# Filling empty TensorE slots with matmuls on a zero tile until the second weight has arrived

## The chip, the cores and the metric

One core of a Trainium2 chip. The metric is the device time of one execution in microseconds (us), the median of several. The profile's span is measured from the first to the last instruction on that core; in the profiled runs here the device time is 1.7 to 2.0 us above it.

Every ratio of two kernels below is the mean time of one kernel's fast runs over the mean time of the other's fast runs in the same rounds on the same chip, so it is not quite the ratio of the medians that are quoted. Brackets hold its 95% interval. A run counts as slow when it is over 1.5% above the fastest run of its kernel.

## The reference

A gated linear recurrence feeds a feed-forward layer with a squared ReLU. Inputs and output are float32.

```python
# q, k, v, alpha: [4 batches, 8 heads, 768 steps, 48]
for t in range(S):
    state = alpha[:, :, t, :, None] * state + einsum('bhd,bhe->bhde', k[:, :, t], v[:, :, t])
    y[:, :, t] = einsum('bhd,bhde->bhe', q[:, :, t], state)
x = y as [3072 tokens, 384]
out = square(relu(x @ w_in)) @ w_out        # w_in [384, 2048], w_out [2048, 384]
```

## The kernel before

The sequence is cut into 24 chunks of 128 steps. A chunk's attention needs four loads (alpha, k, q, v) and a chain across engines: decay sums on TensorE, exponentials on ScalarE, scaled q and k on VectorE, transposes, scores, mask, result, transposition into `XT`. The feed-forward layer takes blocks of chunks: `s1` (into `psH`, weight `WIN`), ReLU on ScalarE, squares shared by VectorE and GpSimd, and `s2` (into `psO`, weight `WOUT`), in four groups of four matmuls per chunk.

No order of instructions is written by hand. The program records operations with a cost, a priority and dependences. A list scheduler inside the kernel plays them through with a small model of the engines and of the two load queues, and its order is what each engine executes, with waits where they are needed.

```python
SHARE = {"sp": 0.25, "pool": 0.75}     # how two load queues share the DMA, in the scheduler's model
...
# GpSimd's queue: four chunks of w_in, then eight of w_out; w_out chunk i is issued when
# the alpha of attention chunk i+1 has landed
W_OUT_FROM = 2
if W_OUT_FROM <= g < W_OUT_FROM + NWO:
    i = g - W_OUT_FROM
    wo_dma[i] = add("pool", w_out_dma(i), 800, -1e4 + i, writes=[("wout", i)], ...,
                    lag=1230, after=[raw_dma[g - 1, "a"]])
...
# s2: four groups of four matmuls; group s needs two of the eight w_out chunks
add("pe", s2, pe_ns(*[DM] * 4), ps_, reads=[("gt", gt, u) for u in us] +
    [("wout", i) for i in range(s * NWO // 4, (s + 1) * NWO // 4)], writes=[("ps", "O")], ...)
# ScalarE copies psO into one of NOSB = 3 output buffers; the out transfer stands in the
# same queue (SP) as the input loads
add("act", lambda e, ob=ob: e.activation(OSB[ob][:], psO[:, 0:DM], AF.Copy), ...,
    reads=[("ps", "O")], writes=[("osb", ob)], name=f"oe{g}")
add("sp", lambda e, ob=ob, r0=r0: e.dma_start(out[r0:r0 + C, :], OSB[ob][:]), 350, ps_ + 1300,
    reads=[("osb", ob)], ...)
```

## Time and profile before

| | before |
|---|---|
| median time | 208.03 us (207.96 to 208.54) |
| span of the profiled run | 204.8 us (this run took 206.55 us, 1.5 us under the median) |
| TensorE busy | 181.4 us, 89% |
| from 60.27 to 202.0 us | TensorE busy 140.44 of 141.73 us |
| clock granted, mean | 0.967 |

How to read it: a high busy share over the whole span hides two regimes, one with holes and one without. The prediction below shows the lines.

### The profile page before, as it was taken

How to read it: one execution, taken by the hardware profiler on the slowest of the kernel's cores; microseconds unless marked ns; L12 is line 12 of the kernel's file. 1: busy time of each engine (PE TensorE's matmuls, PEld its weight loads, DVE VectorE, ACT ScalarE, POOL GpSimd, SP SyncE). 2: the span in 40 equal slices, each digit the busy share in tenths (PEclk: the TensorE clock that was granted, in tenths of full speed). 3: DMA queues.
4: the chain of work that ended last, by engine and by line, in shares of the span. 5: the costliest groups of instructions: out<-in, count | busy, mean ns of one | idle time of the engine just before them, and what ended most of it. 6: DMA issues, size and time to landing. Idle time of an engine off the chain costs nothing.

```text
span 204.8 us, 4675 instructions
## 1 busy us (share of the span) xinstructions
PE 181.4 (89%) x1940; PEld 136.0 (66%) x1940; DVE 110.8 (54%) x175; ACT 111.4 (54%) x237; POOL 89.4 (44%) x113
## 2 busy tenths in 40 slices
PE   1375597698699999999999999999999999999984
PEld 0275486486576677777767778778777786777752
DVE  4433546578875536835274575656845847643200
ACT  3125336467585446743574846756847657455540
POOL 8305325249565227324624446626527334223440
PEclk9999559799999999999999999999999999999999
DMA  6999999999999999999497394081011110110112
GB/s 129 167 198 184 182 219 223 200 206 194 211 187 178 207 192 214 196 229 241 113 191 158 82 226 118 17 180 38 3 38 42 38 42 0 43 38 0 42 38 77
DMA packets 107093, 27.04 MB, mean 132 GB/s; under 512 B 100416, under 2 KB 107072, under 8 KB 107072
## 3 DMA queue, kind: packets, MB, share of 16 engines
q1 hardware_dynamic: 103296, 23.60, 53.5%
q0 software_dynamic: 3776, 3.15, 10.6%
q8 instruction: 15, 0.25, 0.5%
q14 instruction: 6, 0.05, 0.1%
HBM read 25.17 MB, written 4.72 MB: 146 GB/s over the span
## 4 chain that ended last, share of the span: by engine, by line
PE 78%; DVE 6%; DMA 6%; ACT 5%; issue 1%; POOL 1%; DVEq 0%; ACTq 0%
PE psO L540 30%; PE psH L518 30%; PE psT L424 6%; DMA wout<-in_moe_w_out_dram 5%; PE psP L436 4%; DVE qks L414 3%; PE psY L452 2%; PE psT L487 2%; DVE pm L441 2%; PE psY L449 1%; DMA raw<-in_alpha_dram 1%; ACT rr L524 1%; PE psA L392 1%; PE psY L465 1%; ACT asb L403 1%
## 5 line engine op out<-in xcount | busy, mean ns | idle before, releaser
L528 POOL TENSOR_TENSOR gt<-rr 128x512 bf16<-128x512 bf16 x48 | 50.2, 1046 | 82.8 <-ACT rr L524 81.5
L524 ACT ACTIVATE rr<-psH 128x512 bf16<-128x512 f32 x96 | 57.4, 599 | 49.3 <-PE psH L518 46.4
L540 PE MATMUL psO<-wout,gt 128*128 128x384 bf16 x384 | 78.2, 330 | 1.4 <-ACT osb L547 0.9
L518 PE MATMUL psH<-xt,win 128*128 128x256 bf16 (+1 forms) x624 | 78.1, 275 | 0.2
L518 PEld LDWEIGHTS psH<-xt,win 128*128 128x128 bf16 x624 | 58.5, 104 | 10.9 <-DVE xt L493 0.5
L540 PEld LDWEIGHTS psO<-wout,gt 128*128 128x128 bf16 x384 | 34.1, 98 | 18.3 <-ACT osb L547 1.4
L528 DVE TENSOR_TENSOR gt<-rr 128x512 bf16<-128x512 bf16 x48 | 22.9, 477 | 27.8 <-ACT rr L524 27.6
L441 DVE TENSOR_TENSOR pm<-psP,ltri 128x1024 bf16<-128x1024 f32 x24 | 29.4, 1223 | 9.1 <-PE psP L436 9.0
L414 DVE TENSOR_TENSOR qks<-raw,asb 128x768 bf16<-128x768 f32 x24 | 25.3, 1057 | 13.6 <-ACT asb L405 13.5
L430 DVE COPY kqt<-psT 128x1024 bf16<-128x1024 bf16 x24 | 16.5, 690 | 9.5 <-PE psT L424 9.0
L493 DVE COPY xt<-psT 128x384 bf16<-128x384 bf16 x24 | 8.5, 355 | 23.9 <-PE psT L487 23.9
L411 POOL CAST vbf<-raw 128x384 bf16<-128x384 f32 x24 | 14.2, 594 | 15.3 <-PE psY L465 9.2
L424 PE MATMUL psT<-ident,qks 128*128 128x128 bf16 x192 | 16.0, 231 | 5.4 <-DVE qks L414 4.2
L424 PEld LDWEIGHTS psT<-ident,qks 128*128 128x128 bf16 x192 | 12.9, 104 | 8.2 <-DVE qks L414 4.5
L547 ACT ACTIVATE osb<-psO 128x384 f32<-128x384 f32 x24 | 11.8, 492 | 11.3 <-PE psO L540 11.0
L459 ACT ACTIVATE xbf<-psY 128x384 bf16<-128x384 f32 x24 | 11.9, 496 | 11.1 <-PE psY L452 11.1
L481 POOL TENSOR_TENSOR sbd<-tmp,acm 128x384 bf16<-128x384 f32 x16 | 14.4, 903 | 6.6 <-DVE tmp L479 6.6
L403 ACT ACTIVATE asb<-psA 128x384 bf16<-128x384 f32 x24 | 11.8, 490 | 9.3 <-PE psA L396 8.2
L388 ACT ACTIVATE lab<-raw 128x384 bf16<-128x384 f32 x24 | 12.9, 538 | 4.0 <-DMA raw<-in_alpha_dram 4.0
L436 PE MATMUL psP<-kqt 64*128 64x128 bf16 x192 | 10.2, 229 | 2.6 <-DVE kqt L430 2.6
L392 PE MATMUL psA<-lab,ltri 128*128 128x384 bf16 x24 | 8.2, 342 | 4.6 <-ACT lab L388 4.4
L452 PE MATMUL psY<-vbf,pm 128*128 128x48 bf16 x192 | 9.0, 186 | 3.4 <-DVE pm L441 3.4
(36 smaller groups left out, 110.5 us busy)
## 6 DMA issues: line engine op xcount, KB each, us to landing
raw<-in_alpha_dram SPq DMA_DIRECT2D x24, 192.0 KB, 4.2
raw<-in_k_dram SPq DMA_DIRECT2D x24, 192.0 KB, 4.0
raw<-in_q_dram SPq DMA_DIRECT2D x24, 192.0 KB, 3.9
raw<-in_v_dram SPq DMA_DIRECT2D x24, 192.0 KB, 4.1
out_dram<-osb SPq DMA_DIRECT2D x24, 192.0 KB, 2.3
win<-in_moe_w_in_dram POOLq DMA_DIRECT2D x4, 384.0 KB, 8.6
wout<-in_moe_w_out_dram POOLq DMA_DIRECT2D x8, 192.0 KB, 4.6
```

Of the source, the lines that this page charges most:

```text
L403: add("act", lambda e: e.activation(ASB[a][:, 0, :], psA[:, 0:HD], AF.Exp, scale=-1.0), act_ns(HD), p0 + 500, reads=[("ps", "A")], writes= ...
L411: add("pool", lambda e: e.tensor_copy(VBF[vb][:], RAW[r][:, 2, :]), 500, p0 + 600, reads=[("raw", r, 2)], writes=[("vbf", vb)], name=f"vc{g}")
L414: add("dve", lambda e: e.tensor_tensor(QKS[qs][:, :, :, 0:D], RAW[r][:, 0:2, :].rearrange("p j (h d) -> p j h d", h=H), ASB[a][:, :, :].re ...
L424: ins = pe.matmul(psT[:, o:o + 128], QKS[qs][:, j, 2 * p:2 * p + 2, :].rearrange("p h d -> p (h d)"), IDENT[:], is_transpose=True)
L430: add("dve", lambda e: e.tensor_copy(KQT[kt][:].rearrange("p j n s -> p (j n s)"), psT[:, :]), dve_ns(1024, 2), p0 + 3000, reads=[("ps", " ...
L436: ins = pe.matmul(psP[:, h, p * 128:(p + 1) * 128], KQT[kt][64 * h:64 * h + 64, 0, p, :], KQT[kt][64 * h:64 * h + 64, 1, p, :])
L441: add("dve", lambda e: e.tensor_tensor(PM[pm][:].rearrange("p j n s -> p (j n) s"), psP[:, :, :].rearrange("p j (n s) -> p (j n) s", n=NPR ...
L481: add("pool", lambda e: e.tensor_tensor(sb3, TMP[g % 2][:].rearrange("p (n d) -> p n d", d=D), acm, ALU.mult), 800, p0 + 8000, reads=[("tm ...
L518: ins = pe.matmul(psH[hb][:, i * n:(i + 1) * n], WIN[:, kk, fj * 128:(fj + 1) * 128], XT[:, kk, g0 * C:g0 * C + n], start=(kk == 0), stop= ...
L524: add("act", lambda e, hb=hb, rb=rb: e.activation(RR[rb][:], psH[hb][:], AF.Relu), act_ns(512), pu + 600, reads=[("ps", "H", hb)], writes= ...
L528: add(eng, lambda e, rb=rb, dst=dst: e.tensor_tensor(dst, RR[rb][:].rearrange("p (i s) -> p i s", i=per), RR[rb][:].rearrange("p (i s) -> ...
L540: ins = pe.matmul(psO[:, 0:DM], GT[gt][:, fj, ti * C:(ti + 1) * C], WOUT[:, fj, :], start=(fj == 0), stop=(fj == FT - 1))
```

## The change

The intent: in the profile before, TensorE's clock fell to half after stretches of 3.41 us in which it was 35% and 46% busy (the prediction shows them), and the start of the kernel is full of short waits. Matmuls on a zero tile, into `psO`, which nothing uses yet, should keep the clock up. They are placed by the scheduler wherever TensorE is free and nothing is ready, as long as TensorE was busy for less than half of the last 3.4 us, and up to the first `s2`. So that this stretch lasts until the second weight is complete, the first `s2` now waits for all eight chunks of it. Three constants of the scheduler's model changed too.

```diff
-    SHARE = {"sp": 0.25, "pool": 0.75}
+    SHARE = {"sp": 0.15, "pool": 0.85}
...
+            if kind == "w" and cold:                       # every 100 ns of the scheduler's time
+                heapq.heappush(events, (now + 100, -1, "w", None))
+                recent = [(a, z) for a, z in recent if z > now - 3400]
+                used = sum(z - max(a, now - 3400) for a, z in recent)
+                if free["pe"] <= now and not avail["pe"] and used < share * 3400:
+                    o = make_warm()
+                    ...                                    # runs now, 216 ns
...
+                    if e == "pe":
+                        recent.append((o.start, o.end))
+                        cold = cold and o.name != last_use
...
+    WARM = nc.alloc_sbuf_tensor("warm", [128, 512], BF16)
+    warmed = add("dve", fill(WARM, 0.0), 200, -3e6, writes=[("warm",)], name="warm")
+    def make_warm():
+        o = Op("pe", lambda pe: pe.matmul(psO[:, 0:512], WARM[:, 0:128], WARM[:]), 216, 0, "w")
...
+    pr.warm = (make_warm, 1000.0, "s2_0_0", 0.5)
...
-    (input loads)  lag=880
+    (input loads)  lag=800
-    reads=[...] + [("wout", i) for i in range(s * NWO // 4, (s + 1) * NWO // 4)]
+    reads=[...] + [("wout", i) for i in range(NWO)]
-    (w_in loads)   lag=2450
+    (w_in loads)   lag=2400
```

Three parts, then: **ZERO** (the zero matmuls), **WAIT** (all of wout before the first `s2`) and **ORDER** (the model's constants, which change nothing on the chip but the order).

More of the change, by code (lines that the diff above doesn't have):

```diff
@@ L39, in __init__ @@
         self.dma_count = {}
+        self.warm = None
     def add(self, eng, fn, cost, prio, reads=(), writes=(), name="", dma=None, lag=0, after=()):
@@ L101, in schedule @@
         tick = 0
+        recent = []
+        cold = self.warm is not None
+        if cold:
+            make_warm, warm_from, last_use, share = self.warm
+            heapq.heappush(events, (warm_from, -1, "w", None))
         def rates():
@@ L122, in schedule @@
             moved = kind in "qm"
+            if kind == "w" and cold:
[4 more added lines that the diff above has]
+                    o = make_warm()
+                    o.start, o.end = now, now + o.cost
+                    o.pos = len(order["pe"])
+                    order["pe"].append(o)
+                    self.ops.append(o)
+                    free["pe"] = o.end
+                    recent.append((o.start, o.end))
+                    done += 1
+                    heapq.heappush(events, (o.end, seq, "f", o))
+                    seq += 1
             if kind == "r":
@@ L151, in schedule @@
                     done += 1
+                    if e == "pe":
+                        recent.append((o.start, o.end))
+                        cold = cold and o.name != last_use
                     if o.sem is not None:
@@ L331, in select @@
                                          pattern=pattern, channel_multiplier=mult)
+    warmed = add("dve", fill(WARM, 0.0), 200, -3e6, writes=[("warm",)], name="warm")
+    def make_warm():
+        o = Op("pe", lambda pe: pe.matmul(psO[:, 0:512], WARM[:, 0:128], WARM[:]), 216, 0, "w")
+        o.deps[warmed] = True
+        o.idx = -1
+        return o
+    pr.warm = (make_warm, 1000.0, "s2_0_0", 0.5)
     for i, t in enumerate(LAB):
@@ L384, in attention @@
             raw_dma[g, nm] = add("sp", lambda e, dst=dst, src=src: e.dma_start(dst, src), 650, p0 - 3 * P + o,
-                                 writes=[("raw", r, j)], name=f"ld{nm}{g}", dma=f"{nm}{r}", lag=880, after=held(g))
+                                 writes=[("raw", r, j)], name=f"ld{nm}{g}", dma=f"{nm}{r}", lag=800, after=held(g))
         lab = LAB[la][:, :, 0:D]
@@ L544, in moe @@
                 us = range(s * nu // 4, (s + 1) * nu // 4)
-                add("pe", s2, pe_ns(*[DM] * 4), ps_, reads=[("gt", gt, u) for u in us] + [("wout", i) for i in range(s * NWO // 4, (s + 1) * NWO // 4)],
+                add("pe", s2, pe_ns(*[DM] * 4), ps_, reads=[("gt", gt, u) for u in us] + [("wout", i) for i in range(NWO)],
                     writes=[("ps", "O")], name=f"s2_{g}_{s}")
@@ L559, in bass_gla_recurrent__then__act_relu_squared_kernel @@
                 wi_dma[i] = add("pool", w_in_dma(i), 800, -1e6 + 3, writes=[("win", i)], name=f"wi{i}", dma=f"wi{i}",
-                                lag=2450)
+                                lag=2400)
         if W_OUT_FROM <= g < W_OUT_FROM + NWO:
```

## The prediction

> **What bounds the kernel now.** I read the page's slices first (its second part), to see where TensorE is full and what clock it was granted. In the slices, each digit is a fortieth of the 204.8 us span, 5.12 us.
>
> ```profile
> span 204.8 us, 4675 instructions
> ...
> PE   1375597698699999999999999999999999999984
> ...
> PEclk9999559799999999999999999999999999999999
> DMA  6999999999999999999497394081011110110112
> ```
>
> TensorE (PE) is full from about 60 us to the end. Before that it has holes, and the clock drops to half in two places. DMA is full from 5 us to about 97 us. So there are two regimes: a start that is paced by loads and dependences, and from 60 us a pure TensorE stretch. The wide stretches confirm it (columns: stretch, length, then busy us of PE, PEld, DVE, ACT, POOL with counts, granted clock, DMA share, GB/s):
>
> ```profile
> 12.06:44.71 32.65, 25.13 (x273) 20.02 (x271) 17.77 (x27) 14.52 (x35) 11.09 (x15) 0.79 1.13 204
> 44.71:60.27 15.56, 12.76 (x171) 10.49 (x172) 11.90 (x17) 11.18 (x26) 11.70 (x14) 1.00 1.10 200
> 60.27:202.00 141.73, 140.44 (x1465) 103.34 (x1465) 75.90 (x120) 82.02 (x173) 60.33 (x67) 1.00 0.47 108
> ```
>
> From 60.27 us on TensorE idles 1.3 us in 141.7. What starts this stretch is in the chain of waits: the last chunk of the second weight, issued late by GpSimd.
>
> ```profile
> 53.81 0.47 DVE tmp L479
> 54.29 0.07 issue
> 54.36 0.77 POOL sbd L481
> 55.13 5.09 DMA wout<-in_moe_w_out_dram
> 60.23 0.05 issue
> 60.27 0.82 PE psO L540 x4
> ```
>
> The reader is to see that the end equals the moment at which wout is complete, plus the TensorE work not yet done by then, plus a tail. The tail is 2.8 us (last matmul ends at 202.0, span 204.8).
>
> The clock. I cut the trace along its transitions, which finer stretches put at 20.99, 31.23, 38.06 and 41.47 us:
>
> ```profile
> 17.58:20.99 3.41, 1.20 (x19) 0.85 (x16) 1.40 (x2) 1.64 (x5) 1.89 (x3) 1.00 1.10 195
> 20.99:24.40 3.41, 1.79 (x25) 1.08 (x22) 2.31 (x3) 1.48 (x5) 0.77 (x1) 0.50 1.06 181
> 24.40:27.82 3.42, 2.76 (x26) 2.55 (x27) 2.13 (x4) 0.47 (x1) 1.37 (x2) 0.50 1.21 220
> 34.64:38.06 3.42, 1.57 (x34) 1.16 (x31) 2.67 (x4) 1.52 (x5) 2.36 (x4) 1.00 1.17 201
> 38.06:41.47 3.41, 3.01 (x23) 2.06 (x21) 1.11 (x3) 1.26 (x4) 0.00 (x0) 0.50 1.26 225
> 51.70:55.12 3.42, 1.78 (x24) 1.54 (x24) 3.17 (x5) 1.26 (x4) 1.79 (x2) 1.00 1.10 209
> ```
>
> A window with 35% busy (1.20 of 3.41) or 46% (1.57) ended the full clock; one with 52% (1.78, the last line) did not. At half clock, 81% (2.76) did not bring it back and 88% (3.01) did. The granted 1.00 of the first 17 us is not to be believed: the 48 matmuls of 128 columns at 12.72 us take 5.15 us, 107 ns each, and those of warm stretches half as much.
>
> **What the Trainium skill says.** "TensorE: Matmul & The Clock Gate", section "Part 1: The HAM clock gate (the "warmup" mystery)": the array starts at half clock and is released or throttled by a free-running window of 3413 ns. The trace agrees: the transitions lie 10.24, 6.83 and 3.41 us apart, that is 3, 2 and 1 windows. The same page's table under "Why this matters for your kernels" warns of idle gaps above about 3 us. Here it is stricter: the clock fell at 38.06 us with no single gap above 1.4 us. "DMA: Bandwidth & Descriptors", section "Issuing engines are not separate DMA queues": loads of all queues share 16 engines and interleave. The trace agrees: the total stays near 200 GB/s whether or not the GpSimd queue is active, so an earlier wout chunk is paid for by the inputs.
>
> **The change, part by part.**
>
> 1. *Zero matmuls.* 42 of them, 128x512, in 17 groups. Cost of one, estimated from 128 columns at 107 ns cold: 428 ns; warm, from 384 columns at 163 ns (four in 0.65 us): 216 ns. So 9.1 us warm, in slots that the scheduler holds empty. The first 8 and the next 6 run cold (up to 6 us) and cover 1.2 to about 7.7 us, so at least one window is above 88% and the clock comes up by about 8 us instead of 17.6. They may delay chunk 0 by about 0.7 us: six cold ones take 2.6 us, and the hole before its transposes is 1.96 us. That is absorbed, because chunk 1's alpha lands only at 12.06 + 4.8 = 16.9 us. After that, TensorE should be a little over half busy, just above the 46 to 52% at which the clock fell or held.
>
> 2. *What the clock is worth.* Busy time at half clock in the kernel before: about 8.9 us up to 17.6, 8.0 us from 21 to 31.2, 3.0 us from 38 to 41.5; half of 19.9 is 10 us. But this is in the start, where loads decide. By walking the order of the changed kernel with the durations of this trace, starting from each alpha's landing (21.6, 27.0, 31.6, 35.0, 40.6, 44.9, 50.0 us for chunks 2 to 8), I find TensorE ahead by about 1 us at 26, 2 us at 33, 3 us at 45. It reaches its first wout matmul at about 51 us.
>
> 3. *The first wout matmul now waits for all eight chunks.* Before, it needed two, and three of the groups of four ran before 60 us (2.0 us of work at 0.65 each). Work done before the wait for the last chunk, from the order and warm durations (128 columns 55 ns, 256 columns 110, 384 columns 163, transposes 57, and so on; the whole kernel is 166.8 us): 28.9 us before, 23.1 us after. So the changed kernel has 5.9 us more left to do when wout is complete.
>
> 4. *wout completes earlier.* GpSimd's order moves: the last chunk's issue stood behind a cast and chunk 5's state product (54.36 us above). Now it stands directly behind chunk 4's state product and the block's last square, some 47 us by my walk. Its other condition is that chunk 8's alpha has landed, 50.0 us in this trace. That landing is bound by bytes: 33 loads of 192 KB, four win chunks of 384 KB and seven wout chunks are 9.4 MB, of which 1.9 MB have moved by 12 us; 7.6 MB at 204 GB/s give 49.2 us, and at 225 GB/s (the fullest window above) 45.8 us. With 5.0 us for issue and landing, wout is complete at 51 to 56 us; I choose 54.
>
> 5. *The sum.* Before: 137.9 us of work left at 60.27 took until 202.0, a ratio of 0.973. After: 143.8 / 0.973 = 147.8 us. Span = 54 + 147.8 + 2.8 = 204.6 us against 204.8. The timed median is 3.2 us above the span (208.03 to 204.8), so 207.8 us. Break-even is wout complete at 54.2 us.
>
> 6. *Queue shares and lags* (0.15/0.85, 800, 2400) only move the scheduler's order; no transfer gets a different rate on the chip.
>
> **Rivals.** (a) *The clock is the bound*: the 10 us of cold excess come off nearly whole, about 199 us. For it: slices 5 and 6 are busy and slow. Against: DMA at 200 GB/s and the two loads-paced waits; freed TensorE time meets data not yet there. I give it little. (b) *The wait for all of wout costs*: TensorE stands at 51 us with no zero matmul left, since they end before the first wout matmul; 3 us idle may throttle it, and the first window of full work then runs at half speed, 1.7 us lost, up to 3.4. With wout at 55 to 56 us the time is 209 to 212. For it: the shared DMA rate. (c) *Loads move up*: the input queue waited 5.3 us for engines between 30 and 50 us (asb, pm, vbf and others); engines 2 to 3 us ahead free buffers sooner, alpha 8 lands near 47 us, wout at 52, the time about 205.5. For it: DMA at 225 GB/s where it was never starved.
>
> **Range and chances.** I take 207.4, between the sum and rival (c), because engines ahead of loads can only help the queue. Range 205.0 to 210.0: wout complete between 51.5 and 55, plus up to a microsecond for a cold restart. Faster than 203.9 needs wout before 50 us, 0.08; slower than 212.2 needs both a late wout and a cold restart, 0.05.
>
> **What would show it.** Step 1: clock 1.00 from about 8 us to the wout wait, or drops to 0.50 where TensorE was below half busy. Step 2: chunk 2's transposes before 25.9 us, first wout matmul's predecessor done near 51 us. Steps 3 and 4: the wait for wout just before the first wout matmul, ending near 54 us, with one to three us of idle. Step 5: TensorE over 98% busy from there to 2.8 us before the end. I am wrong if wout lands well before 52 us, if the input loads run clearly faster than 204 GB/s, or if TensorE is starved again after wout.

## The result

The changed kernel took 214.25 us (212.9 to 215.2, four runs) against 208.25 us (207.96 to 208.54) of the kernel before: ratio 1.0284 [1.0225, 1.0342], slower. The prediction of 207.4 us, with 205.0 to 210.0, was wrong.

The slices of the changed kernel, one fortieth being 5.3 us:

```profile
span 212.6 us, 4761 instructions
...
PE   7787685893999995999999999999999999999984
...
PEclk9999799698599997999999999999999999999999
DMA  6999999999999989947909729244010000100001
```

TensorE is busier at the start, but it stays full only from the eleventh slice, at full clock from the twelfth, and there is a new hole in the sixteenth, with the clock at 0.7 in it. In stretches (columns: stretch, length, busy us of PE, PEld, DVE, ACT, POOL with counts, granted clock, DMA share, GB/s):

```profile
11.57:48.57 37.00, 28.30 (x341) 20.73 (x340) 22.67 (x31) 18.52 (x42) 17.37 (x20) 0.91 1.06 190
48.57:59.06 10.49, 6.93 (x57) 4.60 (x58) 6.75 (x8) 3.65 (x10) 4.98 (x7) 0.67 1.07 191
59.06:79.71 20.65, 20.65 (x210) 14.48 (x207) 10.27 (x16) 10.75 (x24) 8.10 (x10) 1.00 1.00 196
79.71:82.21 2.50, 0.01 (x1) 0.00 (x1) 0.51 (x1) 0.54 (x2) 0.01 (x1) 1.00 0.98 233
82.21:85.60 3.39, 3.39 (x13) 1.96 (x14) 0.42 (x1) 1.03 (x2) 0.00 (x0) 0.50 1.00 246
85.60:209.80 124.20, 123.56 (x1314) 92.26 (x1312) 67.51 (x106) 73.38 (x154) 55.00 (x59) 1.00 0.36 85
```

The first line holds the loads: 190 GB/s, where the kernel before had 204. The first wout matmul starts at 59.06 us, not at 54. Then the stretch of full work is broken at 79.71 us for 2.5 us, and the next 3.39 us run at half clock, which costs half of them, 1.7 us. The chain of waits tells what broke it (start, length, what):

```profile
78.01 0.30 ACT rr L559
78.31 3.27 DMA out_dram<-osb
...
81.67 0.50 ACT osb L582
...
82.21 1.46 PE psO L575 x4
```

Read backwards: TensorE could not write `psO` before ScalarE had copied the fourth output out of it; ScalarE had no free output buffer; and the first out transfer, whose data had been ready since 63.8 us, was issued only at 78.31 us, because in the one queue of the SP engine it stood behind input loads. This is how the input queue and ScalarE looked (timeline: start, length, engine, line, operation; in brackets the idle time before and its releaser):

```profile
63.32 0.49 ACT L582 ACTIVATE osb<-psO 128x384 f32<-128x384 f32 x1 [0.16 <-PE psO L575]
...
73.73 0.49 ACT L582 ACTIVATE osb<-psO 128x384 f32<-128x384 f32 x1 [1.04 <-PE psO L575]
81.67 0.49 ACT L582 ACTIVATE osb<-psO 128x384 f32<-128x384 f32 x1 [3.06 <-DMA out_dram<-osb]
```

```profile
76.68 0.66 SPq L419 DMA_DIRECT2D raw<-in_alpha_dram  x1
77.38 0.89 SPq L419 DMA_DIRECT2D raw<-in_v_dram  x1
78.31 1.15 SPq L585 DMA_DIRECT2D out_dram<-osb  x1
79.51 0.43 SPq L419 DMA_DIRECT2D raw<-in_v_dram  x1
```

In the kernel before, the first out transfer stood in that queue just as long (copied at 61.13 us, issued at 76.32 us), but its order did other work there: the fourth copy came at 80.81 us, when the buffer was free again.

```profile
71.10 0.49 ACT L547 ACTIVATE osb<-psO 128x384 f32<-128x384 f32 x1
80.81 0.48 ACT L547 ACTIVATE osb<-psO 128x384 f32<-128x384 f32 x1
```

So the span divides as 59.06 us to the first wout matmul, 146.5 us of work after it (209.79 less 59.06, less 2.50 and 1.70), 2.5 us of stall, 1.7 us lost to the clock and a tail of 2.8 us: 212.6. Against the 204.6 us of the prediction's sum, the first term is 5.1 us longer, the second 1.3 us shorter, and the stall with its half clock, 4.2 us, was not in the sum.

That is a reading of one trace. The experiments ask three questions: which part of the change brings the loss; is the stall at 80 us on the path that sets the end; and why is the first wout matmul late, and does that matter?

### The profile page after: what moved, and what is told of

Same layout as the page of the kernel before. It is cut to its first block, busy times and chain, and to the rows that moved or that the text cites.

```text
span 212.6 us, 4761 instructions
## 1 busy us (share of the span) xinstructions
PE 191.8 (90%) x1982; PEld 137.7 (65%) x1982; DVE 113.6 (53%) x176; ACT 111.6 (52%) x237; POOL 92.1 (43%) x113
## 4 chain that ended last, share of the span: by engine, by line
PE 77%; SPq 9%; DMA 8%; ACT 2%; POOL 2%; DVE 1%; issue 1%; POOLq 0%; ACTq 0%
PE psO L575 30%; PE psH L553 28%; SPq L419 9%; PE psT L459 5%; DMA win<-in_moe_w_in_dram 4%; PE psP L471 3%; DMA raw<-in_alpha_dram 3%; PE psT L522 2%; PE psY L487 2%; PE psY L484 2%; PE psA L427 2%; DMA out_dram<-osb 2%; PE psY L500 2%; DVE gt L563 1%; PE psO L361 1%; ACT osb L582 1%
## 5 line engine op out<-in xcount | busy, mean ns | idle before, releaser
L563 POOL TENSOR_TENSOR gt<-rr 128x512 bf16<-128x512 bf16 x48 | 51.5, 1073 | 78.3 <-ACT rr L559 75.6
L553 PE MATMUL psH<-xt,win 128*128 128x256 bf16 (+1 forms) x624 | 77.1, 270 | 1.1 <-DMA win<-in_moe_w_in_dram 0.7
L553 PEld LDWEIGHTS psH<-xt,win 128*128 128x128 bf16 x624 | 56.6, 100 | 13.6 <-ACT rr L559 1.7
L575 PEld LDWEIGHTS psO<-wout,gt 128*128 128x128 bf16 x384 | 34.6, 98 | 19.9 <-ACT osb L582 3.7
L563 DVE TENSOR_TENSOR gt<-rr 128x512 bf16<-128x512 bf16 x48 | 26.6, 554 | 34.4 <-ACT rr L559 34.3
L449 DVE TENSOR_TENSOR qks<-raw,asb 128x768 bf16<-128x768 f32 x24 | 24.3, 1014 | 15.5 <-ACT asb L440 15.3
L446 POOL CAST vbf<-raw 128x384 bf16<-128x384 f32 x24 | 15.5, 645 | 17.8 <-PE psY L500 11.4
L361 PE MATMUL psO<-warm 128*128 128x512 bf16 x42 | 15.7, 488 | 1.3 <-DVE warm L352 1.3
L471 PEld LDWEIGHTS psP<-kqt 64*128 64x128 bf16 x192 | 5.5, 95 | 10.6 <-DVE kqt L465 6.1
```

The source lines that it names most:

```text
L361: o = Op("pe", lambda pe: pe.matmul(psO[:, 0:512], WARM[:, 0:128], WARM[:]), 216, 0, "w")
L446: add("pool", lambda e: e.tensor_copy(VBF[vb][:], RAW[r][:, 2, :]), 500, p0 + 600, reads=[("raw", r, 2)], writes=[("vbf", vb)], name=f"vc{g}")
L449: add("dve", lambda e: e.tensor_tensor(QKS[qs][:, :, :, 0:D], RAW[r][:, 0:2, :].rearrange("p j (h d) -> p j h d", h=H), ASB[a][:, :, :].re ...
L471: ins = pe.matmul(psP[:, h, p * 128:(p + 1) * 128], KQT[kt][64 * h:64 * h + 64, 0, p, :], KQT[kt][64 * h:64 * h + 64, 1, p, :])
L553: ins = pe.matmul(psH[hb][:, i * n:(i + 1) * n], WIN[:, kk, fj * 128:(fj + 1) * 128], XT[:, kk, g0 * C:g0 * C + n], start=(kk == 0), stop= ...
L563: add(eng, lambda e, rb=rb, dst=dst: e.tensor_tensor(dst, RR[rb][:].rearrange("p (i s) -> p i s", i=per), RR[rb][:].rearrange("p (i s) -> ...
```

## The experiments

### One part at a time

Each of the three parts was put into the kernel before alone, and in pairs. The scheduler then makes a new order each time, so parts need not add up.

**f_order**: only the constants.

```diff
-    SHARE = {"sp": 0.25, "pool": 0.75}
+    SHARE = {"sp": 0.15, "pool": 0.85}
-    lag=880 / lag=2450
+    lag=800 / lag=2400
```

> Kernel before with only the queue shares (0.15/0.85) and the lags (800, 2400) of the change, so only the order of instructions differs; no zero matmuls, wout waited for in pairs. Theory ORDER (the new order makes each input chunk share its loads with a wout chunk, inputs arrive later, and out-transfers queue behind inputs): 211 to 214 us, chunk 8's alpha issued after 47 us. Theory WAIT (the wait for all of wout costs) and theory ZERO (the zero matmuls cost): 207 to 209 us.

**f_wait**: only the wait.

```diff
-    [("wout", i) for i in range(s * NWO // 4, (s + 1) * NWO // 4)]
+    [("wout", i) for i in range(NWO)]
```

> Kernel before with only the wait of the first wout matmul for all eight wout chunks. Theory WAIT: 211 to 214 us, first wout matmul after 58 us with an idle TensorE in front of it. ORDER and ZERO: 207 to 210 us.

**f_zero**: the changed kernel with the old wait and the old constants; 34 zero matmuls.

> Kernel before with only the zero matmuls (34 of them, as the first wout matmul comes earlier there). Theory ZERO (they hold TensorE when real work is ready): 210 to 213 us. ORDER and WAIT: 205 to 208 us, clock up from about 8 us.

**f_wait_order**: the changed kernel without the line `pr.warm = ...`.

> Changed kernel scheduled without zero matmuls (wait for all of wout and new shares and lags). ZERO: 207 to 210 us. ORDER or WAIT: 212 to 216 us.

**f_zero_order**: the changed kernel with the old wait.

> Changed kernel with the wait for wout in pairs as before (zero matmuls and new shares and lags, 33 zero matmuls). WAIT: 205 to 209 us. ORDER: 211 to 215 us. ZERO: 211 to 215 us.

**f_zero_wait**: the changed kernel with the old constants.

> Changed kernel with the old shares and lags (zero matmuls and the wait for all of wout). ORDER: 206 to 209 us. WAIT or ZERO: 211 to 215 us.

| parts present | ratio to before | longest wait of TensorE for a copy out of psO after 60 us |
|---|---|---|
| none (before) | 1 | 0.6 us |
| ZERO | 0.986 [0.977, 0.995] | 0.7 us |
| WAIT | 1.011 [1.005, 1.017] | 0.6 us |
| ORDER | 1.013 [1.006, 1.020] | 3.7 us (profile of a slow run) |
| ZERO, WAIT | 1.007 [1.004, 1.010] | 2.4 us |
| ZERO, ORDER | 1.016 [1.009, 1.022] | 2.9 us |
| WAIT, ORDER | 1.011 [1.007, 1.015] | 1.7 us |
| all three (changed) | 1.028 [1.023, 1.034] | 2.5 us |

The medians were 210.91 us (f_order), 210.29 (f_wait), 206.79 (f_zero), 210.12 (f_wait_order), 211.72 (f_zero_order) and 208.91 (f_zero_wait). No single-cause theory fits all six. ORDER came nearest: it named f_zero, f_zero_order and f_zero_wait and missed f_order and f_wait by 0.1 and 0.3 us, but it fails in f_wait_order (212 to 216 us expected), and alone it is 1.3% of the 2.8%. ORDER and WAIT each cost about one per cent alone, below what their theories named (211 to 214 us). ZERO alone gains: its own theory, that the zero matmuls are in the way, is refuted there. But two of the four runs of f_zero count as slow, so its ratio rests on two; and its real work also has a new order, so the gain is not shown to be the clock's. And no sum of parts gives 1.028: what counts is the order that comes out. The right-hand column, read off the traces afterwards, shows one thing that the slower orders tend to share, and f_wait one that is slower without it: there the first wout matmul came at 62.4 us, as expected, though 210.29 us was less than expected.

### The zero matmuls taken out of the changed order

**x_drop**: the order of every engine exactly that of the changed kernel, the zero matmuls not emitted.

```diff
+        order["pe"] = [o for o in order["pe"] if o.name != "w"]   # after scheduling
+        self.ops = [o for o in self.ops if o.name != "w"]
```

> Changed kernel in exactly its order on every engine, but the 42 zero matmuls are left out when the program is written. ZERO: 208 to 210 us, faster than the changed kernel by 4 us or more. ORDER or WAIT: 213 to 217 us, no faster than the changed kernel; slower by the half-clock time of the first 17 us if the zero matmuls help at all.

214.36 us, ratio 1.0265 [1.017, 1.036]; its profile is of a slow run. The changed kernel has 1.0284, and 1.0269 when it was run again (below). In this order the 42 zero matmuls neither help nor harm within about 1%, though without them the mean clock of the fast runs was 0.943 to 0.944 and with them 0.958 to 0.976; the loss sits in the order and its waits. So much for the prediction's hope and for theory ZERO alike.

### Is the stall at 80 us on the path?

**x_osb6**: six output buffers instead of three. The order of instructions on all five engines is the same as that of the changed kernel; only the waits for a free buffer move.

```diff
-    ... NGT, NOSB = 6, 2, 3, 3, 3, 2, 4, 2, 4, 7, 3
+    ... NGT, NOSB = 6, 2, 3, 3, 3, 2, 4, 2, 4, 7, 6
```

> Changed kernel with six instead of three output buffers; TensorE's order up to the first wout matmuls is the same. The stall of 2.5 us at 79.7 us (TensorE waits for the copy out of psO, that for a free output buffer, that for an out transfer standing behind inputs in the queue) and the half clock after it (1.6 us lost) should go: 210 us, 4 us faster than the changed kernel. If the stall was not on the path that sets the end: 213 to 215 us.

208.86 us, ratio 1.0077 [1.0048, 1.0106]. The profile was of a slow run, so it was run once more.

> Changed kernel in exactly its order, six output buffers, again: 1.004 to 1.011 of the kernel before. In the profile TensorE waits under 1 us for the copy out of psO after 60 us, and the span is the time of the first wout matmul plus 147.8 plus 2.8 us, within 1 us.

209.43 us, ratio 1.0087 [1.0049, 1.0124], profile of a fast run. **Some 2% of the 2.8% are the stall.** The other 0.8% was not taken apart: it fits the work that WAIT moves behind wout (f_wait alone costs 1.1%), but the changed kernel with six buffers and the old wait was not run. Waits of TensorE after 60 us, in the changed kernel from 70 us and in x_osb6_b from 60 us (engine, line, releaser: us in total, times, longest):

```profile
PE psO L575 <- ACT osb L582: 3.1, 2, 2.5
```

```profile
PE psO L575 <- ACT osb L582: 0.6, 1, 0.6
```

The same copy now goes straight on at 77.72 us, into a fourth buffer (timeline of ScalarE in x_osb6_b):

```profile
77.72 0.49 ACT L582 ACTIVATE osb<-psO 128x384 f32<-128x384 f32 x1
```

Its first wout matmul starts at 58.11 us and its last matmul ends at 204.48 us, 146.4 us later: the same work as in the changed kernel once the stall and the half clock are taken off (146.5). The expected formula with 147.8 us would have given 208.7; the span is 207.3. That misses the 1 us that was allowed for: the term for the work was 1.4 us too long.

**x_outact**: three buffers as before, but ScalarE issues the out transfer right behind its copy, so that it no longer stands behind inputs.

```diff
-    SHARE = {"sp": 0.15, "pool": 0.85}
+    SHARE = {"sp": 0.15, "pool": 0.85, "act": 0.15}
-            add("sp", lambda e, ob=ob, r0=r0: e.dma_start(out[r0:r0 + C, :], OSB[ob][:]), ...
+            add("act", lambda e, ob=ob, r0=r0: e.dma_start(out[r0:r0 + C, :], OSB[ob][:]), ...
```

> Changed kernel with its three output buffers, but each out transfer is issued by ScalarE's queue right behind the copy and so does not stand behind inputs. OUTQUEUE: the 2.5 us stall falls below 1 us and the time is 4 us below the changed kernel, ratio 1.003 to 1.012. If the number of buffers is the cause and not the queue: ratio 1.02 or more.

211.37 us, ratio 1.0099 [1.0064, 1.0135]. Ten of its 19 runs count as slow, so the median is that of a slow run, as is the profile, and the ratio rests on the other nine. The longest wait is 0.6 us again, with three buffers. It is therefore the place of the out transfers in the queue, not the number of buffers as such, that made the stall; more buffers only outlast it. (TensorE's order differs from the changed kernel's from the fourth output chunk on, where chunk 9's decay sums move back and an `s1` group moves up, so just before the place of the stall; this run is less exact than x_osb6.)

**before_osb6**: the kernel before with six buffers.

> Kernel before with six output buffers. Theory OUTQUEUE (the changed order reaches its fourth output while the first out transfer still stands behind inputs; before, the fourth output came after it): no gain here, 0.99 to 1.005 of the kernel before, as before lost only 0.9 us there. If three buffers cost both kernels alike: 0.975 to 0.985.

205.62 us, ratio 0.9864 [0.9817, 0.9912]: not what the theory expected. But here the scheduler used the buffers for a new order. So the same was done with the order kept.

**b_osb6_same**: scheduled with three buffers, emitted with six.

```diff
     pr.schedule()
+    for i in range(3, len(oes)):
+        del oes[i].deps[outs[i - 3]]
+        if i >= 6:
+            oes[i].deps[outs[i - 6]] = True
     pr.place()
```

> Kernel before in exactly its order on every engine, with six output buffers. If the wait for a free output buffer costs the kernel before too: 0.984 to 0.990. If only the order that came with six buffers was better: 0.995 to 1.002.

207.63 us, ratio 1.0014 [0.9981, 1.0047]. In its own order the kernel before loses nothing to its three buffers. The stall belongs to the changed order; the gain of before_osb6 came from a different order, and what is better in that one was not looked into.

### Why the first wout matmul is late, and what it is worth

In the changed kernel TensorE stood idle twice before it, and the clock fell: 1.35 us before chunk 5's decay sums (waiting for its alpha) and 3.47 us before chunk 5's scores. The second is in TensorE's timeline:

```profile
47.88 0.62 PE L459 MATMUL psT<-ident,qks 128*128 128x128 bf16 x8
51.97 0.61 PE L471 MATMUL psP<-kqt 64*128 64x128 bf16 x8 [3.47 <-DVE kqt L465]
```

and its cause in VectorE's: a square of 0.43 us took 2.13 us, in front of the copy that the scores need, while GpSimd ran a product and a square at 49.19 and 49.98 us.

```profile
49.18 2.13 DVE L563 TENSOR_TENSOR gt<-rr 128x512 bf16<-128x512 bf16 x1 [0.44 <-ACT rr L559]
51.24 0.68 DVE L465 COPY kqt<-psT 128x1024 bf16<-128x1024 bf16 x1
```

```profile
49.19 0.84 POOL L516 TENSOR_TENSOR sbd<-tmp,acm 128x384 bf16<-128x384 f32 x1
49.98 1.04 POOL L563 TENSOR_TENSOR gt<-rr 128x512 bf16<-128x512 bf16 x1
```

On the other side, wout: its last chunk was issued at 53.48 us, when chunk 8's alpha had landed, and took 5.2 us to issue and land, so it was there at about 58.7 us. Two theories: ARRIVAL (wout sets the moment) and CHAIN (TensorE's own late work sets it). The next four were run together.

**after_again**: the changed kernel, unchanged.

> The changed kernel as it is, on the chip of the three kernels that follow, so that these can be compared with it: 212 to 216 us, 1.02 to 1.035 of the kernel before.

213.92 us, ratio 1.0269 [1.0197, 1.0340].

**x_nogate**: wout issued without waiting for an alpha.

```diff
     pr.schedule()
+    for o in wo_dma.values():
+        o.deps.clear()
     pr.place()
```

> Changed kernel in its order, but GpSimd issues the wout chunks without waiting for an input chunk's alpha to land (it stood idle for 0.8 to 2.5 us each time). Theory ARRIVAL (the first wout matmul is late because wout is complete only at 58.2 us): wout complete by 54 us, first wout matmul at 55 to 57 us, 2 to 3 us faster. Theory CHAIN (it is late because TensorE's own work in front of it is late): first wout matmul at 58 to 60 us if inputs are not hit, later if the earlier wout chunks delay them; time within 1 us of the changed kernel.

213.28 us, ratio 1.0289 [1.0230, 1.0349]. A miss as a test: GpSimd works its list in order, so its last wout chunk was still issued only at 52.22 us, behind casts that wait for inputs, and the first wout matmul came at 58.79 us. It shows that the gate on alpha alone was not what held wout back.

**x_fill**: 5 and 16 more zero matmuls in the two idle stretches.

> Changed kernel in its order, with 5 more zero matmuls before chunk 5's decay sums and 16 more before chunk 5's scores, where TensorE stood idle 1.35 and 3.47 us and the clock then fell. It keeps the clock up from 38 to 58 us. CHAIN with the clock as its main part: first wout matmul 2 to 3 us earlier and the time 1 to 3 us lower. ARRIVAL: TensorE is ready earlier but waits for wout until about 58 us, under 1 us lower.

212.98 us, ratio 1.0179 [1.0104, 1.0254], from two fast runs of four; profile of a slow run. The first wout matmul came 1.4 us earlier than in after_again (57.59 and 59.00 us), and the stall at 80 us grew from 2.6 to 3.3 us.

**x_memset**: GpSimd's four squares of block 2 replaced by fills with zero. Its output is wrong, which doesn't matter for the time.

```diff
-            add(eng, lambda e, rb=rb, dst=dst: e.tensor_tensor(
+            add(eng, (lambda e, dst=dst: e.memset(dst, 0.0)) if eng == "pool" and m == 2
+                else lambda e, rb=rb, dst=dst: e.tensor_tensor(
```

> Changed kernel in its order with a wrong result on purpose: GpSimd's four squares of block 2 (128x512) are fills with zero, same waits, same outputs. Theory CONTENTION (two VectorE squares took 2.56 and 2.13 us instead of 0.43 because GpSimd's squares ran at the same time): these two fall below 0.8 us, the 3.47 us wait of TensorE for VectorE's copy falls below 1.5 us, first wout matmul 1 to 4 us earlier unless wout's landing holds it. Rival (VectorE's squares are slow by themselves or wait for something else): they stay above 2 us.

213.72 us, ratio 1.0300 [1.0242, 1.0358]. VectorE's four squares of that block took 0.43, 0.42, 0.41 and 1.10 us; the 1.10 is above the expected 0.8 and ran beside GpSimd's state product, the one operation of that stretch which still reads two tiles:

```profile
47.38 1.10 DVE L563 TENSOR_TENSOR gt<-rr 128x512 bf16<-128x512 bf16 x1 [0.58 <-ACT rr L559]
```

```profile
47.34 0.84 POOL L516 TENSOR_TENSOR sbd<-tmp,acm 128x384 bf16<-128x384 f32 x1
48.12 0.53 POOL L563 MEMSET gt<- 128x512 bf16 x1
```

TensorE's wait fell from 3.47 to 1.91 us, above the expected 1.5 us. CONTENTION is supported: "SBUF — State Buffer", section "SBUF: two separate sides", says that a port pair shared by VectorE and GpSimd is an exclusive lock, which also a VectorE operation with two SBUF inputs needs against a GpSimd operation that reads SBUF; the 2.13 us here beside 0.43 agree. The first three squares overlapped no fill, so they only show the time of a square alone. The times of ending say more: in the lines above the slow square ends at 51.31 us, 0.29 us after GpSimd's second operation; here it ends at 48.48 us, 0.30 us after the product and in the middle of a fill. So VectorE waited for what reads tiles, for two such operations in a row if need be, and not for the fill. The first wout matmul came 1.6 us earlier (57.39 us), and the time did not move: the stall was 3.7 us.

So x_fill and x_memset brought the first wout matmul forward, and the stall took 0.7 and 1.1 us of that back. The output path was the next gate.

**x_osb6_fill**: six buffers and the fill of x_fill.

> Changed kernel with six output buffers and the 21 extra zero matmuls of x_fill. OUTQUEUE (the stall swallowed the 1.4 us that x_fill gained at the first wout matmul): about 1.4 us below six buffers alone, ratio to the kernel before 1.000 to 1.003. If the start does not set the end: as six buffers alone, 1.006 to 1.010.

209.41 us, ratio 1.0049 [1.0020, 1.0079], against 1.0077 and 1.0087 without the fill: a difference of 0.3%, inside the intervals, and between the two expectations. Its profile is the clearest of the series. The clock was 1.000 over the whole span, and still the span is 207.4 us where x_osb6_b, with 0.76 from 51.5 to 58.5 us, had 207.3. TensorE was ready and waited for wout (chain of waits in x_osb6_fill; the wait for wout was 0.7 us):

```profile
48.23 4.57 DMA raw<-in_alpha_dram
52.80 0.29 issue
53.08 5.05 DMA wout<-in_moe_w_out_dram
58.13 0.05 issue
58.18 0.82 PE psO L575 x4
```

ARRIVAL holds for this step: with the clock kept up, the first wout matmul is at 58.18 us, and in x_osb6_b without it at 58.11 us. In the changed kernel CHAIN and ARRIVAL end within half a microsecond of each other (59.06 and about 58.7 us). The chain that leads to it is inputs (chunk 8's alpha, issued at 48.2 us) and then wout. In the kernel before that alpha was issued at 44.71 us, in the profile of the changed kernel at 48.57 us. By the stretches shown, 0.37 MB more had moved by then since chunk 1's alpha (37.00 us at 190 GB/s against 32.65 us at 204): six wout chunks had gone ahead instead of five, and a seventh was issued 0.16 us before it. At 200 GB/s that is 1.9 us of the 3.9 us. The rest is the lower rate, but **the rate is not a mark of the new order**. b_osb6_same has exactly the order of the kernel before, and in its profile, of a fast run, the same stretch looks like this:

```profile
11.49:46.24 34.75, 26.57 (x281) 21.09 (x282) 18.51 (x27) 15.56 (x37) 12.10 (x16) 0.75 1.07 192
```

So the old order took 32.65 and 34.75 us from chunk 1's alpha to chunk 8's; in fast profiles the changed order took 37.00 us, 34.54 (after_again, 195 GB/s), 34.59 (x_memset, 199) and 36.23 (x_osb6_b, 194). A part of the 3.9 us is therefore chance of the two profiles compared. What moves the rate from run to run was not settled.

### A version that beats both

**f_zero_osb6**: the zero matmuls alone, with six buffers.

> Kernel before with only the zero matmuls, and six output buffers: 0.98 to 0.99 of the kernel before, the best of these kernels; the zero matmuls' own gain is about 1%, the buffers add at most 0.5%.

205.52 us, ratio 0.9879 [0.9833, 0.9925]. It beats both kernels, as do f_zero (0.986, two fast runs) and before_osb6 (0.986), each by less than 2%. The two do not add up: each gives about 1.4%, together 1.2%.

## Why the prediction was wrong

- **What bounds the kernel** was right: the end is the first moment at which TensorE becomes full plus the work left. The formula worked where no new stall came: x_osb6_b and the changed kernel have 146.4 and 146.5 us of work after the first wout matmul, against 147.8 predicted.
- **Step 1, the zero matmuls**: the early half was right: chunk 0's scores at 8.8 us took 0.40 us, the warm duration. The second half was wrong. "A little over half busy" did not hold: the clock dropped three times before 59 us, after stretches of 3.41 us that were 45%, 38% and 12% busy (ending at 24.2, 37.9 and 51.5 us). The longest waits in them were for chunk 2's alpha (1.3 us), for chunk 3's mask on VectorE and then chunk 5's alpha (1.1 and 1.4 us), and for a VectorE copy (3.47 us). (The matmuls stand in 16 groups, not 17.)
- **Step 2, what the clock is worth**: the claim that most of it is hidden behind loads was right and is shown by x_osb6_fill, with a full clock and no gain. Its number was wrong: TensorE came to the first wout matmul at 59 us, not 51. My walk used the landings of the kernel before and VectorE durations without GpSimd beside them; alpha 5 landed at 37.6 instead of 35.0 us, and one square of 2.13 us was followed by half clock. That is not all of the 8 us: with a full clock x_osb6_fill was still ready only at 57.4 us, and the remainder was not traced.
- **Step 3, 5.9 us more to do**: near. TensorE's busy time after the first wout matmul, the half clock taken off, was 145.9 us against 140.4, 5.5 us more; with fewer holes the time for it was 146.5 against 141.7 us, 4.8 more.
- **Step 4, wout complete at 54 us**: wrong, about 58.7 us, outside its 51 to 56. The mechanism (alpha 8 and then 5 us) was right; the size failed in when alpha 8 lands, 53.4 instead of 49.2 us. The rate was 190 and not 204 to 225 GB/s, and the prediction's own byte count at 190 gives 52 us. It had the rate from one profile, and the old order itself was seen at 192.
- **Step 5, the sum**: it had no term for a stall after wout, because the kernel before had none. "I am wrong if [...] TensorE is starved again after wout" is what happened: 2.5 us of stall and 1.7 us of half clock. x_osb6 shows it as the larger share of the loss, about 2% of 2.8%. The step that failed is that I read the order only up to the first wout matmul. The orders of TensorE and of the input queue were both available; counting outputs against out transfers in the queue would have shown three outputs done while the first transfer still stood behind inputs. Its last term was too long as well: 3.2 us compare a median with the span of another run. The profiled run took 206.55 us, 1.75 us above its span, so 1.5 of the 3.2 us are the difference between runs; without them the sum is 206.4 us.
- **Rivals**: (a), 10 us off, did not come. (b) named a standstill followed by half clock, and this did come, but at another place, the output buffers, and not at the wait for wout. (c) had the sign of the loads wrong: in the profile they came later, not earlier.

## What to carry to other kernels

When a change makes a scheduler write a new order, follow every queue of the new order to its end and ask at each buffer who frees it; a transfer behind others in a queue can be harmless in one order and a stall in the next. A faster clock brought nothing in a stretch whose end was set by a load (x_osb6_fill): find what the next full stretch waits for before filling holes. And to separate a wait from the order that comes with it, keep the schedule and change only the buffers or the emitted instructions, as x_osb6, b_osb6_same and x_drop do.

## What the Trainium skill lacked or had wrong

- "TensorE: Matmul & The Clock Gate" warns of idle gaps above about 3 us and tells of one kernel whose short idles between bursts also brought the clock down, but it names no busy share. Here the clock fell at 38.06 us in the kernel before without a gap above 1.4 us, in a window that was 46% busy; 52% kept it. In the changed kernel a window with 45% (up to 24.20 us) ended the full clock and one with 56% (31.03 to 34.44 us) did not.
- The same page says that the throttle has two values on a core alone, and that it has been seen stuck at a quarter. One of four runs of f_order took 427.55 us: the clock was 1.00 from 100 to 160 us and 0.16 from 170 us to the end, 255 us long, with TensorE busy for 252 of them. The other three took 210.31 to 210.98 us.
- "SBUF — State Buffer" gives the lock between VectorE and GpSimd, and a slowdown of VectorE without its operations, but not how long a wait can get. Here a 128x512 square of 0.43 us took 2.13 and 2.56 us, and ended 0.29 us after the last of two and of three GpSimd operations in a row that read tiles.
- "DMA: Bandwidth & Descriptors" tells that the queues share the engines, but not how far the rate of the same transfers differs between executions; here the same order of two queues moved at 204 GB/s in one fast run and at 192 in another. No run settled why.
